# Row dot products for wq on VectorE, wq loaded in halves at its first use, and a kept group's slots spread, in a decode backward kernel

## The chip, the cores and the metric

The kernel runs on one core of one Trainium2 chip. The metric is device time in microseconds (us). A verdict of faster or slower needs 2%; intervals (95%) are given and used.

## The reference

Two layers of attention over a cached K and V and of an MLP, forward and backward, for one decoded token and a batch of 2. Cut to what matters:

```python
B, Sq, D = 2, 1, 1024
Hq, Hkv, Sk, Dh = 32, 4, 16384, 128          # 8 query heads share one KV head
q = (x @ wq)...                              # wq: 1024 x 4096
scores = einsum("bhqd,bhkd->bhqk", q, k) * Dh ** -0.5
o = einsum("bhqk,bhkd->bhqd", softmax(scores), v);   out = o.reshape(B, Sq, -1) @ wo
# x = x + A(layernorm(x)); x = x + B(layernorm(x)); both twice; then jax.vjp of all of it
```

The change lies in the attention backward of layer 1. For each of 8 groups g (batch row b, KV head kv; g = 4b + kv) it streams V (dP = dO V^T), makes dS, streams K (dq = dS K), and when both batch rows of a KV head have their dq, it adds that head's part of dn = dq wq^T.

## The kernel before

All weights, V and K pass through one pool of 1 MB tiles, `ld`, with NLD = 7 buffers. The last group (G - 1) keeps its K and V on chip, so its slots load nothing. A slot handles a quarter of a chunk: 8 transposes of 128x128 tiles of V, the 8 score matmuls of two slots earlier, and in every other slot 8 dq matmuls with K.

```python
slots = []
for i, g in enumerate(groups):                 # 0, 4, 3, 7, 1, 5, 2, 6
    for c in range(NCH):                       # 4 chunks of 1 MB
        for b in range(NB):                    # 4 slots to a chunk
            if g != G - 1:
                slots.append((g, c, b))
            if groups[(i + 1) % G] == G - 1:   # kept group beside the one before it
                slots.append((G - 1, c, b))
...
def finish(ps, g=g):                           # dq of group g is ready
    V.tensor_scalar(out=dqT[:, g, :], in0=ps, scalar1=QSCALE, scalar2=None, op0=ALU.mult)
    if groups.index(g) % 2 == 1:               # second batch row of a head
        wq_n[g % HKV][1]()                     # dq into dq_all
        if g != groups[-1]:
            wq_q.append(wq_n[g % HKV][3])      # the head's product, behind what is queued
        else:
            wq_n[g % HKV][3]()
...
if groups.index(g) % 2 == 1 and b == 1 and c == 1:
    n = wq_n[g % HKV] = wq_steps(...)
    for f in n[0]:                             # both halves of the head's wq: 2 x 1 MB, from ld
        f()
    wq_q.extend(n[2])                          # 8 row turns
...
if wq_q and s % 2 == 1:                        # one queued item in every other slot
    wq_q.popleft()()
```

A turn is 8 TensorE transposes of a 128x1024 row block and the copy back over it; the product then takes 8 row blocks x 8 matmuls of 32 columns. Copies out of PSUM (evacuations) go to ScalarE or VectorE, whichever has less booked in the balancer `load`; `charge` books time there:

```python
def pick():
    m = min(load.values())
    for k in load:
        load[k] -= m
    return "A" if load["A"] <= load["D"] else "D"
```

Of the kernel before, what the change touches and what calls it, by code (L numbers as in the profile page):

```python
# [9 lines left out]
BF16 = mybir.dt.bfloat16  # L10
F32 = mybir.dt.float32
I32 = mybir.dt.int32
ACT = mybir.ActivationFunctionType
ALU = mybir.AluOpType
# [9 lines left out]
def kernel(  # L24
# [25 lines left out]
    V = nc.vector  # L50
    S = nc.scalar
    PE = nc.tensor
# [39 lines left out]
    def pt(shape, dtype, name):  # L92
        return ps_tp.tile(shape, dtype, name=name, tag="tp")

    def px(shape, dtype, name):
        return ps_x.tile(shape, dtype, name=name, tag="x")
# [4 lines left out]
    def pm_(shape, dtype, name):  # L101
        return ps_sm.tile(shape, dtype, name=name, tag="sm")
# [34 lines left out]
    def charge(eng, us):  # L137
        load[eng] += us
# [7 lines left out]
    def evac_bf16(dst, src, n):  # L146
        if pick() == "A":
            S.copy(out=dst.bitcast(I32), in_=src.bitcast(I32))  # L148
            charge("A", 0.17 + n / 2 / 1200.0)
        else:  # L150
            V.tensor_copy(out=dst, in_=src)  # L151
            charge("D", 0.16 + n / 1920.0)
# [163 lines left out]
    class Ahead:  # L316
# [7 lines left out]
        def load(self, k):  # L324
            j0, rb = self.chunks[k]
            wv = w_load(self.W, j0, rb, D)
            for j in range(rb):
                self.rows[j0 + j] = wv[:, j, :]
# [9 lines left out]
        def products(self, j, out_ps, gT_bf):  # L338
            for o in range(8):
                PE.matmul(wide_out(out_ps, 2 * j), lhsT=self.rows[j][:, o * 128:(o + 1) * 128],  # L340
                          rhs=wide_in(gT_bf[:, o, :]), start=(o == 0), stop=(o == 7))
# [42 lines left out]
    class Acc:  # L384
# [3 lines left out]
        def __init__(self, g, src, coef, finish, half=0):  # L388
            self.g, self.src, self.coef, self.finish = g, src, coef, finish
            self.pre = {}  # L390
            self.cv = None
            self.acc = ACCT[:, half * 256:half * 256 + 256]
            self.half = half
            zero = lambda: V.memset(self.acc, 0.0)
            if half in Acc.in_use:
                Acc.then[half] = zero
            else:
                zero()
            Acc.in_use.add(half)
# [152 lines left out]
    def attn_bwd(l, do_bf, dqT, dn, groups, ahead):  # L552
        sch = Sched()
        wq_q, wq_n, w2_q = deque(), {}, deque()
        slots = []
        for i, g in enumerate(groups):
            for c in range(NCH):
                for b in range(NB):
                    if g != G - 1:
                        slots.append((g, c, b))  # L560
                    if groups[(i + 1) % G] == G - 1:
                        slots.append((G - 1, c, b))
        kTs, sc, accs = {}, {}, {}
        made = {"n": 0}

        def post(g, c):
            dp = sc.pop((g, c))
            PE.matmul(dp[:].rearrange("p h t -> p (h t)"), lhsT=hot3[:],
                      rhs=dlr[:, g, l, :].unsqueeze(2).to_broadcast([128, 8, TC]), start=False, stop=True)
            k = made["n"]  # L570
            made["n"] += 1
            ds = dXr[k // 2 % 3][:, :, k % 2]
            ev = e_all[:, g, c * CP:(c + 1) * CP, l, :, :].rearrange("p a h b -> p h a b")
            V.tensor_tensor(out=ds.rearrange("p a h b -> p h a b"),
                            in0=dp[:].rearrange("p h (a b) -> p h a b", b=2), in1=ev, op=ALU.mult)
            charge("D", 0.5)
            if c == 0:
                def finish(ps, g=g):
                    V.tensor_scalar(out=dqT[:, g, :], in0=ps, scalar1=QSCALE, scalar2=None, op0=ALU.mult)
                    if groups.index(g) % 2 == 1:  # L580
                        wq_n[g % HKV][1]()
                        if g != groups[-1]:
                            wq_q.append(wq_n[g % HKV][3])
                        else:
                            wq_n[g % HKV][3]()
                accs[g] = Acc(g, "K", None, finish, groups.index(g) % 2)
            acc = accs[g]
            if g == groups[-1]:
                accs[g].pre[c] = kv_load("K", g, c)
                if c == NCH - 1:  # L590
                    for k in range(NLD - 2):
                        ahead.load(k)
                        j0, rb = ahead.chunks[k]
                        w2_q.extend(lambda j=j: ahead.row(j) for j in range(j0, j0 + rb))
            coef = lambda u: ds[:, u - c * CP].rearrange("p h t -> p (h t)")
            sch.later(2, lambda: queue_acc(sch, acc, [c], c == NCH - 1, coef))

        def score(s):
            g, c, b = slots[s]
            if b == 0:  # L600
                sc[g, c] = px([128, 8, TC], F32, "dp")
            kT = kTs.pop(s)
            for j in range(8):
                PE.matmul(sc[g, c][:, :, b * 8 + j], lhsT=kT[:, j, :], rhs=do_bf[:, g, :], start=(b + j == 0),
                          stop=False)
            if b == NB - 1:
                post(g, c)

        cv = None
        s = 0  # L610
        v_turns = deque(lambda c=c, b=b: turn(held_tiles["V%d" % c][:, b * 1024:(b + 1) * 1024],
                                              lambda: pt([128, 8, 128], BF16, "turn"))
                        for c in range(NCH) for b in range(NB))
        while s < len(slots) + 2 or sch.busy():
            sch.s = s
            if s < len(slots):
                g, c, b = slots[s]
                if g == G - 1:
                    kTs[s] = kept_vT(c)[:, b * 8:(b + 1) * 8, :]
                else:  # L620
                    if b == 0:
                        cv = kv_load("V", g, c)
                    kTs[s] = emit_T(cv, b, True)
                    if s % 2 == 1 and v_turns:
                        v_turns.popleft()()
                if groups.index(g) % 2 == 1 and b == 1 and c == 1:
                    n = wq_n[g % HKV] = wq_steps(l, g % HKV, dqT, dn, lambda: pt([128, 8, 128], BF16, "wtq"),
                                                 lambda: px([128, 512], F32, "dn_ps"))
                    for f in n[0]:
                        f()  # L630
                    wq_q.extend(n[2])
            sch.run_slot(1 if s < len(slots) else 2)
            if 2 <= s < len(slots) + 2:
                score(s - 2)
            if wq_q and s % 2 == 1:
                wq_q.popleft()()
            s += 1
        return w2_q


# [148 lines left out]
    def wq_steps(l, kv, dqT, dn, new_tp, new_ps, get_=None, done_=lambda *job: None):  # L789

        hs = slice(kv * 8, kv * 8 + 8)
        box = {}

        def load(j):
            wt = ld.tile([128, LDW], BF16, name="wqt", tag="ld") if get_ is None else get_("wq", kv, j)
            box[j] = wt[:].rearrange("p (j n) -> p j n", j=4)
            if get_ is None:
                nc.sync.dma_start(box[j], wq_v[:, j:j + 4, kv * D:(kv + 1) * D])

        def turn_row(j):  # L800
            turn(box[j - j % 4][:, j % 4, :], new_tp)

        def products():
            ps = new_ps()
            for j in range(DJ):
                for o in range(8):
                    PE.matmul(wide_out(ps, 2 * j), lhsT=box[j - j % 4][:, j % 4, o * 128:(o + 1) * 128],  # L807
                              rhs=wide_in(dq_all[:, kv * 8 + o, 2 * l:2 * l + 2]), start=(o == 0), stop=(o == 7))
            V.tensor_tensor(out=dn[:], in0=dn[:], in1=ps[:, 0:2 * DJ].rearrange("p (j b) -> p j b", b=2), op=ALU.add)
            for j in (0, 4):  # L810
                done_("wq", kv, j)

        def dq_in():
            for b in range(2):
                V.tensor_copy(out=dq_all[:, hs, 2 * l + b], in_=dqT[:, b * HKV + kv, :])

        return [lambda j=j: load(j) for j in (0, 4)], dq_in, [lambda j=j: turn_row(j) for j in range(DJ)], products

    def attn_in_bwd(l, gT, dn, hook=lambda: None):
        sv = saved[f"a{l}"]  # L820
# [21 lines left out]
    fps = px([128, 512], F32, "w2b_f")  # L842
    V.memset(fps[:, 0:DJ * WIDE], 0.0)
    w2b = Ahead(B_w2, F, "w2b", h_all[:, :, lsl(1)], fps)
    rest = attn_bwd(1, do1, dq1, dn1, [b * HKV + kv for kv in (0, HKV - 1, *range(1, HKV - 1)) for b in range(2)], w2b)

    for k in range(NLD - 2, len(w2b.chunks)):
        w2b.load(k)
# [466 lines left out]
```

## Time and profile before

| | before |
|---|---|
| median (range) | 1181.85 us (1181.4 to 1183.74), 3 runs |
| layer-1 attention backward, by the trace | 512.8 us (dO in bf16) to 684.0 us (dn complete) |
| TensorE, VectorE, ScalarE, share of the span | 83%, 51%, 46% |
| mean HBM traffic | 379 GB/s; 413 to 423 in the best slices |

A row of the windows view lists busy us of PE (matmul), PEld (weight load), DVE (VectorE), ACT (ScalarE) and POOL, each with its number of instructions in brackets, then the granted TensorE clock, the DMA share, and GB/s. A row of the waits view reads "who and line <- what ended the wait: us in all, times, longest". The lines themselves are in the prediction.

### The profile page before, as it was taken

How to read it: one execution, taken by the hardware profiler on the slowest of the kernel's cores; microseconds unless marked ns; L12 is line 12 of the kernel's file. 1: busy time of each engine (PE TensorE's matmuls, PEld its weight loads, DVE VectorE, ACT ScalarE, POOL GpSimd, SP SyncE). 2: the span in 40 equal slices, each digit the busy share in tenths (PEclk: the TensorE clock that was granted, in tenths of full speed). 3: DMA queues.
4: the chain of work that ended last, by engine and by line, in shares of the span. 5: the costliest groups of instructions: out<-in, count | busy, mean ns of one | idle time of the engine just before them, and what ended most of it. 6: DMA issues, size and time to landing. Idle time of an engine off the chain costs nothing. (4 is left out here: it accounts for less than half of the span.)

```text
span 1179.9 us, 40673 instructions
## 1 busy us (share of the span) xinstructions
PE 975.0 (83%) x17981; PEld 750.0 (64%) x17981; DVE 606.4 (51%) x1262; ACT 539.1 (46%) x1368; POOL 63.9 (5%) x113
## 2 busy tenths in 40 slices
PE   4988894487879976899978689888898889999786
PEld 3866673487767755888767588755555554555452
DVE  1544351233545423454323235557777878786774
ACT  0544341022535420344323234357767767786673
POOL 0000000000000000000000000001111111111111
PEclk9988795597989875899989899978767877786785
DMA  9999999989999989989899999767999999999996
GB/s 370 415 417 417 417 417 395 395 337 364 418 417 416 414 311 416 371 322 380 316 396 398 365 335 368 287 236 279 394 407 413 418 417 421 419 420 420 423 423 269
DMA packets 89133, 449.35 MB, mean 381 GB/s; under 512 B 7026, under 2 KB 7026, under 8 KB 49788
## 3 DMA queue, kind: packets, MB, share of 16 engines
q1 hardware_dynamic: 72204, 348.17, 74.5%
q0 software_dynamic: 16752, 98.59, 20.3%
q8 instruction: 140, 2.29, 0.8%
q14 instruction: 37, 0.30, 0.1%
HBM read 348.14 MB, written 98.58 MB: 379 GB/s over the span
## 5 line engine op out<-in xcount | busy, mean ns | idle before, releaser
L148 ACT COPY kT<-tp 128x512 int32<-128x512 int32 x176 | 103.4, 588 | 272.3 <-PE tp L379 263.0
L151 DVE COPY kT<-tp 128x1024 bf16<-128x1024 bf16 x192 | 131.3, 691 | 153.7 <-PE tp L379 143.1
L379 PE MATMUL tp<-ident,kv_K 128*128 128x128 bf16 x1728 | 145.8, 234 | 3.6 <-DMA kv_K<-in_A_k_cache_dram 3.6
L379 PEld LDWEIGHTS <-kv_K 128*128 128x128 bf16 x1728 | 110.6, 104 | 4.4 <-DMA kv_K<-in_A_k_cache_dram 4.1
L156 ACT CAST big<-xm 128x512 bf16<-128x512 f32 (+1 forms) x163 | 88.9, 593 | 26.5 <-PE xm L976 14.4
L159 DVE CAST big<-xm 128x512 bf16<-128x512 f32 (+1 forms) x134 | 87.2, 685 | 23.7 <-PE xm L1117 10.9
L532 PEld LDWEIGHTS <-kT 128*128 128x128 bf16 x2048 | 76.4, 98 | 28.1 <-issue 22.0
L532 PE MATMUL sc<-qT_bf,kT 128*128 128x8 bf16 x2048 | 92.0, 171 | 0.5 <-issue 0.4
L263 PE MATMUL wtp<-ident,wt 128*128 128x128 bf16 x928 | 77.4, 232 | 5.3 <-issue 4.0
L297 PEld LDWEIGHTS <-wt 128*128 128x128 bf16 x1696 | 49.0, 104 | 46.7 <-issue 14.9
L496 ACT ACTIVATE e_all<-sc,negm 128x64 bf16<-128x64 f32 x256 | 77.2, 345 | 1.1 <-DVE negm L491 1.1
L379 PE MATMUL tp<-ident,kv_V 128*128 128x128 bf16 x864 | 68.2, 223 | 6.2 <-DMA kv_V<-in_A_v_cache_dram 4.0
L411 PE MATMUL acc_all<-kv_V,e_all 128*16 128x256 bf16 x864 | 46.3, 294 | 29.4 <-DMA kv_V<-in_A_v_cache_dram 16.1
L159 DVE CAST keepK<-xm 128x512 bf16<-128x512 f32 x93 | 60.4, 685 | 18.2 <-PE xm L1117 14.0
L148 ACT COPY wT<-wtp 128x512 int32<-128x512 int32 (+1 forms) x60 | 34.3, 572 | 71.8 <-PE wtp L263 62.2
L151 DVE COPY wT<-wtp 128x1024 bf16<-128x1024 bf16 (+1 forms) x64 | 40.7, 640 | 51.1 <-PE wtp L263 47.5
L156 ACT CAST keepK<-xm 128x512 bf16<-128x512 f32 x104 | 56.2, 592 | 21.7 <-PE xm L1117 20.6
L263 PEld LDWEIGHTS <-wt 128*128 128x128 bf16 x928 | 59.4, 104 | 5.9 <-issue 4.5
L156 ACT CAST keepV<-xm 128x512 bf16<-128x512 f32 (+1 forms) x93 | 50.4, 594 | 24.7 <-PE xm L1117 22.6
L159 DVE CAST keepV<-xm 128x512 bf16<-128x512 f32 (+1 forms) x79 | 51.8, 685 | 16.2 <-PE xm L1117 12.4
L496 ACT ACTIVATION_READ_ACCUMULATOR e_all<-sc,negm 128x1 f32 x256 | 60.1, 235 | 0.0
L379 PEld LDWEIGHTS <-kv_V 128*128 128x128 bf16 x864 | 53.4, 100 | 7.7 <-DMA kv_V<-in_A_v_cache_dram 4.4
(325 smaller groups left out, 1758.0 us busy)
## 6 DMA issues: line engine op xcount, KB each, us to landing
kv_K<-in_A_k_cache_dram SPq DMA_DIRECT2D x81, 1024.0 KB, 13.1
kv_V<-in_A_v_cache_dram SPq DMA_DIRECT2D x81, 1024.0 KB, 12.2
out_dram<-big POOLq DMA_DIRECT2D x36, 1024.0 KB, 15.8
wt<-in_A_wo_dram SPq DMA_DIRECT2D x32, 1024.0 KB, 10.3
wt<-in_B_w_dram SPq DMA_DIRECT2D x32, 896.0 KB, 14.3
out_dram<-keepK POOLq DMA_DIRECT2D x22, 1024.0 KB, 15.8
out_dram<-keepV POOLq DMA_DIRECT2D x18, 1024.0 KB, 16.2
wt<-in_A_wq_dram SPq DMA_DIRECT2D x16, 1024.0 KB, 9.2
```

The lines of the kernel that those rows point to most:

```text
L148: S.copy(out=dst.bitcast(I32), in_=src.bitcast(I32))
L151: V.tensor_copy(out=dst, in_=src)
L156: S.copy(out=dst, in_=src)
L159: V.tensor_copy(out=dst, in_=src)
L263: PE.transpose(tp[:, o, :], wv[:, j, (o0 + o) * 128:(o0 + o + 1) * 128], ident[:])
L297: PE.matmul(fps[:, jo, :].rearrange("p (a b) -> p a b", b=2), lhsT=wv[:, j, jo * 128:(jo + 1) * 128], rhs=xT_bf[:, j0 + j, :].unsqueeze(1) ...
L379: PE.transpose(tp[:, j, :], cv[:, b * 8 + j, :], ident[:])
L411: PE.matmul(self.acc[cg:cg + 16, :], lhsT=coef(u), rhs=self.cv[:, t:t + 2, :].rearrange("p t d -> p (t d)"), start=False, stop=True, tile_ ...
L496: S.activation(out=e_all[:, g, f * half:(f + 1) * half, l, h, :], in_=sc[g][f][:, h, :].rearrange("p (a b) -> p a b", b=2), func=ACT.Exp, ...
L532: PE.matmul(sc[g][f][:, :, t % TH], lhsT=kT[:, j, :], rhs=q_bf[:, g, :], start=True, stop=True)
```

## The change

The intent: take wq work off TensorE, which looks full, and give it to VectorE, which is half idle; and hold load buffers for wq for less time. Five of the eight half-heads (20 of 32 row blocks) become dot products on VectorE. Each half is loaded when its first dot or turn is emitted. The kept group's slots are spread over two groups and it gets an accumulator of its own. With more than six wq items queued, one is taken in every slot instead of in every other one.

```diff
-                    if g != G - 1:
-                        slots.append((g, c, b))
-                    if groups[(i + 1) % G] == G - 1:
-                        slots.append((G - 1, c, b))
+                    slots.append((g, c, b))
+                    if 2 <= i < 2 + NCH // 2 and c % 2 == 0:
+                        slots.append((G - 1, (i - 2) * 2 + c // 2, b))
...
+        def dot(kv, n, j, b):
+            V.scalar_tensor_tensor(out=junk[:], in0=n[4][j - j % 4][:, j % 4, :], scalar=1.0,
+                                   in1=dqb[b][:].rearrange("p o d -> p (o d)"), op0=ALU.mult, op1=ALU.mult,
+                                   accum_out=dnp[:, kv, j, b:b + 1])
+            charge("D", 1.15)
+            if b == 1:
+                V.tensor_tensor(out=dn[:, j], in0=dn[:, j], in1=dnp[:, kv, j], op=ALU.add)
+        def spread(kv, b):          # dq of one batch row to all partitions: 8 transposes, 1 copy
...
+        def by_dots(kv):            # called when both batch rows of a head have their dq
+            nj = DJ // 2 if kv == groups[-3] % HKV else DJ      # head 1: half on TensorE
...
+            def item(j, b):
+                if j % 4 == 0 and b == 0:
+                    n[0][j // 4]()  # load this half now
+                dot(kv, n, j, b)
...
-                    if groups.index(g) % 2 == 1:
+                    done_g.append(g % HKV)
+                    if g == groups[-1]:
                         wq_n[g % HKV][1]()
-                        if g != groups[-1]:
-                            wq_q.append(wq_n[g % HKV][3])
-                        else:
-                            wq_n[g % HKV][3]()
-                accs[g] = Acc(g, "K", None, finish, groups.index(g) % 2)
+                        wq_n[g % HKV][3]()
+                    elif done_g.count(g % HKV) == 2:
+                        by_dots(g % HKV)
+                accs[g] = Acc(g, "K", None, finish, 2 if g == G - 1 else groups.index(g) % 2)
...
-            if wq_q and s % 2 == 1:
+            if wq_q and (s % 2 == 1 or len(wq_q) > 6):
                 wq_q.popleft()()
+            if dots and s % 3 < 2:
+                dots.popleft()()
```

More of the change, by code (lines that the diff above doesn't have):

```diff
@@ L391, in __init__ @@
             self.cv = None
-            self.acc = ACCT[:, half * 256:half * 256 + 256]
+            self.acc = ACCT[:, half * 256:half * 256 + 256] if half < 2 else pm_([128, 256], F32, "acc2")[:]
             self.half = half
@@ L558, in attn_bwd @@
                 for b in range(NB):
-                    if g != G - 1:
-                        slots.append((g, c, b))
-                    if groups[(i + 1) % G] == G - 1:
-                        slots.append((G - 1, c, b))
+                    slots.append((g, c, b))
+                    if 2 <= i < 2 + NCH // 2 and c % 2 == 0:
+                        slots.append((G - 1, (i - 2) * 2 + c // 2, b))
         kTs, sc, accs = {}, {}, {}
         made = {"n": 0}
+        done_g = []
+        dots = deque()
+        dqb = [ktp.tile([128, 2 * NB, 128], BF16, name="dqb", tag="blk", bufs=2) for _ in range(2)]
+        junk = wrk.tile([128, D], BF16, name="junk", tag="rowout")
+        dnp = vec.tile([128, HKV, DJ, 2], F32, name="dnp")
+        def dot(kv, n, j, b):
[6 more added lines that the diff above has]
+        def spread(kv, b):
+            tp = pt([128, 8, 128], BF16, "dqr")
+            for o in range(8):
+                PE.transpose(tp[:, o, :], dq_all[:, kv * 8 + o, 2 * l + b:2 * l + b + 1].to_broadcast([128, 128]), ident[:])
+            evac_bf16(dqb[b][:].rearrange("p a b -> p (a b)"), tp[:].rearrange("p a b -> p (a b)"), 1024)
+        def by_dots(kv):
+            n = wq_n[kv] = wq_steps(l, kv, dqT, dn, lambda: pt([128, 8, 128], BF16, "wtq"),
+                                    lambda: px([128, 512], F32, "dn_ps"))
+            nj = DJ // 2 if kv == groups[-3] % HKV else DJ
+            n[1]()
+            for b in range(2):
+                wq_q.append(lambda b=b: spread(kv, b))
+            def item(j, b):
+                if j % 4 == 0 and b == 0:
+                    n[0][j // 4]()
+                dot(kv, n, j, b)
+            wq_q.append(lambda: dots.extend(lambda j=j, b=b: item(j, b) for j in range(nj) for b in range(2)))
+            if nj < DJ:
+                wq_q.append(lambda: (n[0][1](), n[2][nj]()))
+                wq_q.extend(n[2][nj + 1:])
+                wq_q.append(lambda: n[3](nj))
         def post(g, c):
@@ L625, in attn_bwd @@
                         v_turns.popleft()()
-                if groups.index(g) % 2 == 1 and b == 1 and c == 1:
+                if g == groups[-1] and b == 1 and c == 0:
                     n = wq_n[g % HKV] = wq_steps(l, g % HKV, dqT, dn, lambda: pt([128, 8, 128], BF16, "wtq"),
                                                  lambda: px([128, 512], F32, "dn_ps"))
-                    for f in n[0]:
-                        f()
-                    wq_q.extend(n[2])
+                    for k, f in enumerate(n[0]):
+                        wq_q.append(lambda f=f, k=k, n=n: (f(), n[2][4 * k]()))
+                        wq_q.extend(n[2][4 * k + 1:4 * k + 4])
             sch.run_slot(1 if s < len(slots) else 2)
@@ L634, in attn_bwd @@
                 score(s - 2)
-            if wq_q and s % 2 == 1:
+            if wq_q and (s % 2 == 1 or len(wq_q) > 6):
                 wq_q.popleft()()
+            if dots and s % 3 < 2:
+                dots.popleft()()
             s += 1
+        assert not dots and not wq_q
         return w2_q
@@ L801, in turn_row, with products @@
             turn(box[j - j % 4][:, j % 4, :], new_tp)
-        def products():
+        def products(j0=0):
             ps = new_ps()
-            for j in range(DJ):
+            for j in range(j0, DJ):
                 for o in range(8):
@@ L808, in products @@
                               rhs=wide_in(dq_all[:, kv * 8 + o, 2 * l:2 * l + 2]), start=(o == 0), stop=(o == 7))
-            V.tensor_tensor(out=dn[:], in0=dn[:], in1=ps[:, 0:2 * DJ].rearrange("p (j b) -> p j b", b=2), op=ALU.add)
+            V.tensor_tensor(out=dn[:, j0:DJ], in0=dn[:, j0:DJ],
+                            in1=ps[:, 2 * j0:2 * DJ].rearrange("p (j b) -> p j b", b=2), op=ALU.add)
             for j in (0, 4):
@@ L815, in dq_in @@
                 V.tensor_copy(out=dq_all[:, hs, 2 * l + b], in_=dqT[:, b * HKV + kv, :])
-        return [lambda j=j: load(j) for j in (0, 4)], dq_in, [lambda j=j: turn_row(j) for j in range(DJ)], products
+        return [lambda j=j: load(j) for j in (0, 4)], dq_in, [lambda j=j: turn_row(j) for j in range(DJ)], products, box
     def attn_in_bwd(l, gT, dn, hook=lambda: None):
@@ L844 @@
     w2b = Ahead(B_w2, F, "w2b", h_all[:, :, lsl(1)], fps)
-    rest = attn_bwd(1, do1, dq1, dn1, [b * HKV + kv for kv in (0, HKV - 1, *range(1, HKV - 1)) for b in range(2)], w2b)
+    rest = attn_bwd(1, do1, dq1, dn1, [b * HKV + kv for kv in (0, HKV - 1, *range(1, HKV - 1)) for b in range(2)
+                                     if b * HKV + kv != G - 1], w2b)
     for k in range(NLD - 2, len(w2b.chunks)):
```

## The prediction

> **What bounds the kernel now.** I started from the page's picture of 40 slices (29.5 us each), to see which stages have the DMA at its ceiling.
>
> ```profile
> PE   4988894487879976899978689888898889999786
> DVE  1544351233545423454323235557777878786774
> DMA  9999999989999989989899999767999999999996
> GB/s 370 415 417 417 417 417 395 395 337 364 418 417 416 414 311 416 371 322 380 316 396 398 365 335 368 287 236 279 394 407 413 418 417 421 419 420 420 423 423 269
> ```
>
> In most slices 413 to 423 GB/s flow: that is the ceiling that this kernel reaches. The attention backward of layer 1, the only place the diff touches, lies at about 513 to 684 us (slices 17 to 23): 316 to 398 GB/s with TensorE at 7 to 9 tenths. So there is something to win here, but only the gap between these rates and the ceiling. Next I cut that stretch into parts, and into pieces of 3 us where the rate was lowest. The columns are the busy us of PE, PEld, DVE, ACT, POOL, the granted clock, the DMA share, and GB/s.
>
> ```profile
> 523.00:580.00 57.00, 54.40 (x1195) 45.78 (x1192) 24.28 (x47) 23.04 (x41) 0.00 (x0) 1.00 0.91 336
> 580.00:664.00 84.00, 65.45 (x1391) 54.14 (x1390) 25.89 (x56) 24.39 (x43) 0.00 (x0) 0.92 1.00 398
> 664.00:679.00 15.00, 14.18 (x287) 11.97 (x287) 5.50 (x10) 5.23 (x10) 0.00 (x0) 0.88 0.89 323
> ```
> ```profile
> 568.00:571.00 3.00, 3.00 (x72) 2.36 (x70) 0.76 (x3) 1.67 (x3) 0.00 (x0) 1.00 0.47 183
> 571.00:574.00 3.00, 3.00 (x77) 2.55 (x73) 1.00 (x3) 1.06 (x2) 0.00 (x0) 1.00 0.33 68
> ```
>
> So the stage has two limits. From 523 to 580 TensorE is busy 54.4 of 57 us and the DMA gets 336 GB/s. From 580 to 664 the DMA is never idle (share 1.00, 398 GB/s), and TensorE waits. VectorE is busy about 43% or less throughout. The DMA's worst hole is 565 to 574 us. The waits of the DMA-issuing queue (490 to 690 us) say what refused it a buffer:
>
> ```profile
> SPq L368 <- PE tp L379: 60.9, 21, 10.8
> SPq L368 <- PE acc_all L411: 49.7, 19, 7.1
> SPq L368 <- PE dn_ps L807: 12.4, 4, 4.6
> ```
>
> L807 is the wq product: four times a K or V load waited for it, since wq shares the seven 1 MB load buffers with K and V. The issue times of wq and the TensorE timeline show how long it keeps them:
>
> ```profile
> 525.59 4.46 SPq L798 DMA_DIRECT2D wqt<-in_A_wq_dram  x2
> 551.67 2.55 SPq L798 DMA_DIRECT2D wqt<-in_A_wq_dram  x2
> ```
> ```profile
> 572.89 0.61 PE L313 MATMUL wtq<-ident,wqt 128*128 128x128 bf16 x8
> 573.33 0.61 PE L379 MATMUL tp<-ident,kv_V 128*128 128x128 bf16 x8
> ...
> 576.56 1.76 PE L807 MATMUL dn_ps<-dq_all,wqt 128*128 128x32 bf16 x64
> 580.04 0.61 PE L379 MATMUL tp<-ident,kv_V 128*128 128x128 bf16 x8 [1.72 <-issue]
> ```
>
> Head 0's two wq buffers are taken at 525.6 and given back after the product at 576.6; head 3's two are taken at 551.7. Between 552 and 577 wq therefore holds four of seven buffers. The code says why: the product is appended to the same queue as the next head's eight turns, and waits behind them (walking the loop by hand: turns in slots 21 to 35, product in slot 59 of 128). The V load behind the pause at 578.3 to 580.0 was issued only at 572.7; at the 7.8 us median that V loads take to land here, it fits. The profile calls this pause "issue", so that reading is mine.
>
> **What the Trainium skill says.** "VectorE: DVE Perf Modes", section "The perf-mode tier table": a bf16 tensor_tensor from SBUF can run at 2x, tensor_reduce at 1x only; it has no row for a scalar_tensor_tensor with an accumulator. I assume 1x. The trace agrees with a 1x slope where it has one: 128x64 f32 tensor_tensor takes 218 ns and 128x256 takes 421 ns, 1.06 ns an element. "TensorE: Matmul & The Clock Gate", section "Back-to-back issue gap", gives about 81 ns per matmul at N=128 in a stream of weight loads and matmuls; this trace is faster (8 transposes start 0.44 us before the next group, 55 ns each), so I use the trace. "Perfetto Trace Analysis", section "Optimization Strategy": consistent bubbles on the engine that should be saturated can mean too few buffers for the next tile. The hole at 565 to 574 us agrees.
>
> **The change part by part.**
> *TensorE, removed.* 20 of 32 wq row blocks lose their turn (8 transposes, 0.44 us) and their product (8 matmuls; a head's 64 take 1.74 us, so 0.22 us): 20 x 0.66 = 13.2 us. *Added:* for three heads and two batch rows, 8 transposes that spread dq over all partitions: 6 x 0.44 = 2.6 us. Net 10.6 us less.
> *Evacuations.* 20 go and 6 come, about 0.6 to 0.7 us each: some 9 us less on ScalarE and VectorE together.
> *VectorE, added.* 20 row blocks x 2 batch rows = 40 dots of 1024 elements. From the 256-element tensor_tensor: 421 + 768 x 1.06 = 1.23 us; the diff itself books 1.15. So 46 to 49 us. VectorE was busy 62.6 of the 170 us from 513 to 683, so it comes to about 110, or 65%. Locally, at most two dots fall in three slots: 2.5 us against three slots of 1.29 us (165 us over 128 slots). With the 0.42 us dS product of every fourth slot that nearly fills it, and the balancer, which is charged for the dots, sends the evacuations to ScalarE (three of 0.59 us in 3.9 us fit).
> *Buffers.* A half is loaded when its first dot or turn is emitted and freed after its last, some 12 slots later. In my walk through the loop, head 0 now holds one buffer in slots 49 to 61 and one in 61 to 72, where heads 0 and 3 had held two to four from slot 21 to 77.
> *Moved.* The 16 slots of the kept group, which load no V or K, were all interleaved with one group (32 slots with little DMA work). They are now spread over two groups (24 slots each), which evens TensorE work per byte. They need a third accumulator; it gets its own PSUM bank, and nothing else here uses that bank.
>
> *On the path.* From 523 to 580 the before moved 336 x 57 = 19.2 MB. At 398 GB/s, the rate of the DMA-bound part next to it, that takes 48.1 us. TensorE must fit under it: 54.4 us, less 16 turns (7.0), less the product and pause (3.4), less some eight kept slots moved to the next group (8 x 0.37 = 3.0), plus two spreads (0.9) gives 42. It fits, so the DMA becomes the bound: 57 - 48.1 = **8.9 us** won. From 580 to 664 nothing is won: same bytes, same rate. The tail (664 to 684) keeps its last loads, eight turns and 64 products of the last head. In my walk the last dot falls in slot 126 of 128, so the dots do not lengthen it. I take off 1 us for dots that hold up an evacuation. Everything later shifts as a block: after 685 us the diff touches nothing. Sum: 1181.85 - 8 = **about 1174 us**.
>
> **The rivals.**
> (1) *VectorE becomes the bound.* A dot waiting for its wq half blocks every evacuation behind it, and TensorE with it. For it: VectorE runs in order, and loads here take 8 to 13 us to land. Against it: V and K too are loaded where they are first used, in the same queue order, so a wq half lands one load (2.6 us) after its neighbour, and there are four transposed-tile buffers. If it held, the gain would shrink to 0 to 4 us: 1178 to 1182, or 1185 at worst.
> (2) *The transfer was the limit anyway.* wq is still 8 MB; if the rate does not rise above 336 GB/s for another reason, little is won: 1179 to 1182. Against it: 398 GB/s right afterwards with the same kind of loads.
> (3) *More than expected.* If the whole stage rose to about 413 GB/s, 523 to 679 (57.5 MB by the 3 us windows) would take 139 instead of 156 us: 17 us, 1165 us. The later part is against it: it stays at 398 with the DMA never idle.
> (4) *The last group gets crowded.* Head 1's wq now falls there too, so it loads 15 MB instead of 13. That is the same total later in the stage; but if the last loads arrive late, 2 to 5 us come back.
>
> **Range and chances.** Even the largest gain, 17 us, is 1.4%, short of 2% (23.6 us). A loss over 2% would need VectorE to hold up nearly every slot. So within 2%: 0.96; faster 0.02; slower 0.02. The range runs from 1167 (most of rival 3) to 1181 (rivals 1 or 4 taking nearly everything).
>
> **What would show it.** (a) The dots take 1.15 to 1.3 us each, 46 to 52 us in all. (b) No wait of a load on the wq product in mid-stage; the hole at 565 to 574 us is gone, and no 3 us window before the tail falls under 250 GB/s. (c) The windows from about 525 us to the tail all show a DMA share near 1.0 and some 400 GB/s. (d) The last wq product, at 682.0 us before, comes at about 674; from there every event is the same 8 us early. The prediction is wrong if the dots wait long for wq with TensorE waiting on VectorE, if the DMA share stays under 0.95 with TensorE busy, or if the gain at the last wq product is lost again after 685 us.

## The result

In the first comparison the changed kernel took 1173.44 us (median of 4 runs, 1170.99 to 1173.91) against 1181.62 us before (4 runs): ratio 0.9929, interval 0.9902 to 0.9955. Two later comparisons gave less: 1176.74 against 1180.31 us (0.9963, 0.9947 to 0.998) and 1179.78 against 1181.35 us (0.997, 0.9941 to 0.9999). So the gain is real but small, 0.3 to 0.7%.

The 40 slices of the changed kernel, for the lines shown of before:

```profile
PE   4988885497879876899987889888898999898886
DVE  1544451133545433454845434567777877886774
DMA  9999999998999989989999989677999999999996
GB/s 370 415 417 416 418 417 396 395 356 351 416 417 413 416 329 416 390 320 398 387 410 411 352 320 338 254 271 322 361 403 419 414 417 421 418 421 418 422 423 263
```

Slices 18 to 21 (counted from 0) carry 387 to 411 GB/s where before had 316 to 398, and VectorE is at 8 tenths in slice 19. The same three windows as in the prediction, and the weakest stretch in mid-stage:

```profile
523.00:580.00 57.00, 54.21 (x1190) 44.80 (x1188) 35.07 (x71) 24.71 (x44) 0.00 (x0) 0.99 0.98 385
580.00:664.00 84.00, 67.10 (x1276) 54.64 (x1274) 42.53 (x98) 38.96 (x71) 0.00 (x0) 0.86 0.99 397
664.00:679.00 15.00, 14.06 (x326) 12.05 (x319) 2.57 (x15) 7.33 (x14) 0.00 (x0) 0.89 0.98 369
```
```profile
565.00:568.00 3.00, 2.70 (x63) 2.19 (x62) 2.96 (x7) 1.48 (x4) 0.00 (x0) 1.00 0.74 243
568.00:571.00 3.00, 3.00 (x77) 2.18 (x73) 2.75 (x7) 1.15 (x2) 0.00 (x0) 1.00 0.90 363
```

The first window rose from 336 to 385 GB/s, with TensorE as busy as before: 54.21 us against 54.40. So TensorE did not get free; it did other work. The same window with only TensorE's instructions on wq (turns and products), before and after, and then with only those that read the loaded V (its transposes), before and after. These rows have one busy column, TensorE's:

```profile
523.00:580.00 57.00, 11.47 (x192) 1.00 0.91 336
523.00:580.00 57.00, 0.00 (x0) 0.99 0.98 385
```
```profile
523.00:580.00 57.00, 19.90 (x262) 1.00 0.91 336
523.00:580.00 57.00, 25.64 (x339) 0.99 0.98 385
```

The 11.5 us of wq work left this window and K and V work took its place. In the trace of before, TensorE waits in these 57 us for only 0.4 us for anything that the profile names. The waits of the DMA-issuing queue (490 to 690 us) show another surprise:

```profile
SPq L368 <- PE acc_all L411: 48.4, 19, 6.8
SPq L368 <- PE tp L379: 47.0, 21, 5.9
...
SPq L368 <- DVE dn L576: 12.7, 5, 4.6
```

K and V loads used to wait 12.4 us for the wq product; they now wait 12.7 us for the last dot of a half (L576 is the sum behind it). The wait changed its owner, not its size (`dn` is the gradient that the dots add into). The dots themselves, from the groups of VectorE instructions from 513 to 690 us:

```profile
L571 DVE SCALAR_TENSOR_TENSOR junk<-wqt,dqb 128x1024 bf16<-128x1024 bf16 x40 | 48.7, 1218 | 5.6 <-DMA wqt<-in_A_wq_dram 5.3
...
L571 DVE DVE_READ_ACCUMULATOR junk<-wqt,dqb 128x1 f32 x40 | 3.3, 82 | 0.0
```

To see where time goes, I cut every trace at the same events: the stage runs from the bf16 copy of dO to the first use of the finished dn; then everything to the end of the span. "DMA idle" sums (1 - share) over the 3 us windows below 1, for 523 to 649 us and for 649 to 682 us.

| trace | stage, us | from there to the end, us | DMA idle mid, us | DMA idle late, us |
|---|---|---|---|---|
| before | 171.2 | 495.9 | 6.8 | 1.9 |
| after (three traces) | 163.9, 166.2, 167.7 | 498.2, 503.1, 501.6 | 2.1, 2.0, 2.8 | 2.3, 5.2, 4.5 |

So the stage is 3.5 to 7.3 us shorter, and part of that is lost again after it, in code that the diff does not touch. In the first pair of traces, whose spans differ by 7.8 us, chance helped: the changed kernel entered the stage 2.8 us earlier (510.0 against 512.8 us), through code that is the same in both.

### The profile page after: what moved, and what is told of

Its sections match the earlier page's. It is cut to its first block, busy times and chain, and to the rows that moved or that the text cites. A ratio compares the mean times of both kernels' runs of the same rounds, so it can differ in the third digit from the quotient of the medians. Undisturbed runs are those within 1.5% of the kernel's fastest.

```text
span 1172.1 us, 40218 instructions
## 1 busy us (share of the span) xinstructions
PE 968.7 (83%) x17709; PEld 743.1 (63%) x17709; DVE 627.2 (54%) x1319; ACT 555.1 (47%) x1395; POOL 63.9 (5%) x113
## 5 line engine op out<-in xcount | busy, mean ns | idle before, releaser
L148 ACT COPY kT<-tp 128x512 int32<-128x512 int32 x204 | 120.0, 588 | 254.5 <-PE tp L379 246.6
L151 DVE COPY kT<-tp 128x1024 bf16<-128x1024 bf16 x164 | 112.1, 690 | 117.1 <-PE tp L379 106.9
L159 DVE CAST big<-xm 128x512 bf16<-128x512 f32 x141 | 91.9, 686 | 33.6 <-PE xm L1018 15.9
L156 ACT CAST big<-xm 128x512 bf16<-128x512 f32 x156 | 84.8, 595 | 24.2 <-PE xm L1018 14.7
L379 PE MATMUL tp<-ident,kv_V 128*128 128x128 bf16 x864 | 72.9, 233 | 9.9 <-DMA kv_V<-in_A_v_cache_dram 8.3
L297 PEld LDWEIGHTS <-wt 128*128 128x128 bf16 x1696 | 48.9, 103 | 45.8 <-issue 14.7
L379 PEld LDWEIGHTS <-kv_V 128*128 128x128 bf16 x864 | 57.5, 104 | 11.8 <-DMA kv_V<-in_A_v_cache_dram 9.2
L156 ACT CAST keepV<-xm 128x512 bf16<-128x512 f32 (+1 forms) x98 | 53.3, 595 | 20.3 <-PE xm L1159 17.0
L159 DVE CAST keepV<-xm 128x512 bf16<-128x512 f32 (+1 forms) x74 | 48.5, 686 | 20.3 <-PE xm L1159 16.1
```

Of the source, the lines that this page charges most:

```text
L148: S.copy(out=dst.bitcast(I32), in_=src.bitcast(I32))
L151: V.tensor_copy(out=dst, in_=src)
L156: S.copy(out=dst, in_=src)
L159: V.tensor_copy(out=dst, in_=src)
L297: PE.matmul(fps[:, jo, :].rearrange("p (a b) -> p a b", b=2), lhsT=wv[:, j, jo * 128:(jo + 1) * 128], rhs=xT_bf[:, j0 + j, :].unsqueeze(1) ...
L379: PE.transpose(tp[:, j, :], cv[:, b * 8 + j, :], ident[:])
```

## The experiments

The change has three parts: **slots** (the kept group spread over two groups), **late halves** (wq loaded in halves where it is first used), and **dots** (VectorE instead of TensorE). My theory by now was that buffers make the gain; the rival, that the relief of TensorE makes it. A third possibility was not given a run of its own: late halves also do the wq work on TensorE later, in a stretch where TensorE has room. The twelve runs went in three calls of four, each run with 5 timed rounds and a profile. All passed the comparison with the reference.

**The changed kernel again.** No edit.

> The changed kernel again, unedited, as the yardstick for the other runs and to see what differs between two traces of one kernel. All theories: 0.5 to 0.9% faster than before (1171 to 1176 us). If the 3 us between 701 and 752 us that the first trace gave back come back here too, they belong to the change; if that stretch takes about 48 us as in the kernel before, they are scatter of one execution.

Measured: 1176.74 us against 1180.31, 0.9963 (0.9947 to 0.998). The first comparison was on the lucky side. After the stage, the stretch from the hidden gradient of layer 0's MLP to the bf16 copy of layer 0's dO (the w1 and wo passes) took 50.9 us in this trace, 51.4 in the first, and 48.3 before. So the 3 us that the first trace lost there were lost again.

**Product first.** The kernel before; a finished head's product goes ahead of the next head's turns.

```diff
-                            wq_q.append(wq_n[g % HKV][3])
+                            wq_q.appendleft(wq_n[g % HKV][3])
```

> The kernel before, with one word changed: a finished head's wq product goes to the front of the queue and not behind the next head's turns, so head 0 gives its two load buffers back some 14 slots (about 14 us) earlier; all work stays on TensorE. Theory buffers (the gain comes from wq no longer holding load buffers): the DMA hole at 565 to 574 us goes and 3 to 5 us of the 8 are won, 1177 to 1179. Rival TensorE work (the gain comes from the 10.6 us of TensorE work taken away): 0 to 1 us won, 1181 to 1182.

Measured: 1178.74 against 1180.31, 0.9985 (0.9967 to 1.0002), not clear of zero. Head 0's product did move, from 576.6 to 561.7 us. The hole of 565 to 574 us did not go; it shrank and spread:

```profile
568.00:571.00 3.00, 3.00 (x73) 2.36 (x71) 0.99 (x2) 1.56 (x3) 0.00 (x0) 1.00 1.03 426
571.00:574.00 3.00, 2.56 (x62) 2.11 (x59) 0.69 (x1) 0.70 (x2) 0.00 (x0) 1.00 0.61 183
574.00:577.00 3.00, 3.00 (x71) 2.34 (x69) 1.45 (x3) 1.56 (x3) 0.00 (x0) 1.00 0.84 322
577.00:580.00 3.00, 3.00 (x79) 2.36 (x76) 1.15 (x2) 0.69 (x2) 0.00 (x0) 1.00 0.82 317
```

Neither theory does well here. Freeing two buffers earlier won little. Two reasons fit, and no run parts them: the buffers were held beside the kept group's slots, which need no loads; and TensorE was full in that stretch (54.7 of 57 us from 523 to 580 us, with the same 128 turn transposes as before), so loads that come sooner find it no freer.

**Slots alone.** The kernel before with the new order of slots and the third accumulator; wq still in early pairs, all on TensorE.

```diff
+                    slots.append((g, c, b))
+                    if 2 <= i < 2 + NCH // 2 and c % 2 == 0:
+                        slots.append((G - 1, (i - 2) * 2 + c // 2, b))
...
+        wq_at = {4: 0, 1: 3, 5: 1, 6: 2}      # group that triggers a head's loads
-                if groups.index(g) % 2 == 1 and b == 1 and c == 1:
+                if g in wq_at and b == 1 and c == 1:
```

> Of the change only the order of slots: the kept group spread over two groups, with its own accumulator; wq as before, loaded early as pairs, turned and multiplied on TensorE. Theory buffers: the spread also takes away the clash of head 0's product with head 3's turns, so 2 to 5 us won, 1177 to 1180. Rival TensorE work: only the evening out helps, 0 to 2 us, 1180 to 1182. If the order of slots is nearly all of the gain: 7 to 8 us, 1174.

Measured: 1188.59 against 1180.31, 1.0067 (1.0042 to 1.0093): 8 us slower, which no theory had expected. The stage took 175.1 us. Its windows (580 to 650 us, and two of 3 us), and what TensorE waited for from 595 to 632 us:

```profile
580.00:650.00 70.00, 56.12 (x1155) 47.17 (x1153) 22.79 (x50) 21.35 (x37) 0.00 (x0) 0.89 0.88 342
606.00:609.00 3.00, 2.21 (x40) 1.73 (x40) 0.00 (x0) 0.59 (x1) 0.00 (x0) 0.81 0.45 156
618.00:621.00 3.00, 2.75 (x56) 2.34 (x56) 1.08 (x3) 1.74 (x3) 0.00 (x0) 1.00 0.39 85
```
```profile
PE acc_all L411 <- DMA kv_K<-in_A_k_cache_dram: 7.4, 3, 3.9
```

The DMA engines stood idle and then TensorE waited for K loads that had been issued late. With the kept group's slots gone from beside them, the early pairs of heads 3 and 1 (issued at 568.8 and 594.8 us) sit in slots that nearly all need K and V (by a walk through the loop, all but four kept slots beside head 3's). That is consistent with the buffers: the place of the holding would matter, not only its length. No run moves the place alone, so this much is argued.

**Slots and late halves, all on TensorE.** The changed kernel without dots: in each half, load, four turns, and the product of those four rows.

```diff
-            for b in range(2):
-                wq_q.append(lambda b=b: spread(kv, b))
-            ... dots.extend(...)
+            for k in range(2):
+                wq_q.append(lambda k=k: (n[0][k](), n[2][4 * k]()))
+                wq_q.extend(n[2][4 * k + 1:4 * k + 4])
+                wq_q.append(lambda k=k: n[3](4 * k, 4 * k + 4))
```

> The changed kernel with all wq work back on TensorE: same slots, same late loads in halves, each half turned and multiplied at once and then given back; no dots on VectorE. Theory buffers: as fast as the change, 1172 to 1175, since the DMA is the bound there. Rival TensorE work: 13 us of TensorE work come back, 4 to 8 us slower than the change, 1178 to 1182.

Measured: 1171.65 against 1180.31, 0.9929 (0.9912 to 0.9946). It is faster than the changed kernel (1176.74). The stage took 165.9 us, as in the changed kernel. All wq work is on TensorE, and the gain is there in full. Against slots alone, only the way that wq is loaded, queued and given back differs, and the two do about the same wq work on TensorE from 523 to 580 us (128 instructions each) at about the same rate (374 and 378 GB/s). The late halves are 17 us faster (1171.65 against 1188.59), and the difference opens from 580 to 650 us: 405 GB/s against 342. So with the new slots the reading that fits is the buffers: loads wait for one while TensorE waits for loads. The parts of late halves (the later load, the return in halves, the faster queue) were not tried one by one.

**Early loads.** The changed kernel with dots and new slots, but both halves of heads 0, 3 and 1 loaded early as before and held.

```diff
-                if j % 4 == 0 and b == 0:
-                    n[0][j // 4]()
...
+                if g in (4, 1, 5) and b == 1 and c == 1:
+                    kv = {4: 0, 1: 3, 5: 1}[g]
+                    n = wq_n[kv] = wq_steps(...)
+                    for f in n[0]:
+                        f()
```

> The changed kernel with one part undone: both halves of a head's wq are loaded together at the points where the kernel before loaded them, and held until the dots are done; the dots stay on VectorE. Theory buffers: two to four of seven buffers are held for long again, so most of the gain goes, or more: 1179 to 1188. Rival TensorE work: the gain stays, 1172 to 1175.

Measured: 1193.93 against 1180.08, 1.0129 (1.0099 to 1.0159), 14 us slower than before although TensorE has its relief. The stage took 181.8 us and 580 to 650 us carries:

```profile
580.00:650.00 70.00, 49.94 (x871) 40.10 (x872) 26.89 (x65) 24.62 (x45) 0.00 (x0) 0.77 0.86 330
```

TensorE is at 71% and the DMA at 0.86; TensorE waits 21.8 us of these 70 for K and V loads. The changed kernel differs only in the late loads. So with the new slots the relief does not carry the gain: without the late loads there is a loss. The relief with the old slots and early loads was not run.

**Old slots.** The changed kernel with the old order of slots (the slot loop, two accumulators and the list of groups as before).

> The changed kernel with the old order of slots (the kept group all beside one group, two accumulators); dots and late halves stay. If the spread of the slots matters for itself: 2 to 4 us slower than the change, 1175 to 1178. If the buffers or the TensorE work alone make the gain: 1172 to 1175.

Measured: 1177.74 against 1180.08, 0.998 (0.9959 to 1.0). The changed kernel, on the same chip, had 0.9963. It was run at another time. By the timed runs that difference is not clear; the stage in the trace is 168.5 us.

**Short dots.** Every dot reads 16 of 1024 elements. The result is wrong (it passed the comparison all the same); loads, waits and bookings stay.

```diff
-            V.scalar_tensor_tensor(out=junk[:], in0=n[4][j - j % 4][:, j % 4, :], scalar=1.0,
-                                   in1=dqb[b][:].rearrange("p o d -> p (o d)"), ...
+            V.scalar_tensor_tensor(out=junk[:, 0:16], in0=n[4][j - j % 4][:, j % 4, 0:16], scalar=1.0,
+                                   in1=dqb[b][:, 0, 0:16], ...
```

> The changed kernel with every dot cut to 16 of 1024 elements (wrong result on purpose, out_1 only or little more), so VectorE loses some 45 us of work; loads and waits for them stay. If the dots hold nothing up (my sum took off 1 us for them): 1172 to 1174. If VectorE has become a bound: 3 to 5 us faster than the change, 1168 to 1170.

Measured: 1176.93 against 1180.08, 0.9962 (0.994 to 0.9984), the same ratio as the changed kernel's. A dot took 166 ns (median), so 42 us of VectorE work were gone, and in 580 to 650 us VectorE fell from 35.15 to 11.25 us at an unchanged DMA rate:

```profile
580.00:650.00 70.00, 56.34 (x1092) 45.67 (x1092) 11.25 (x74) 31.44 (x57) 0.00 (x0) 0.85 1.02 411
```

So the dots' own time holds nothing up that these runs can resolve.

**Dots twice.** The same kernel with every dot done twice.

```diff
+            for _ in range(2):
                 V.scalar_tensor_tensor(out=junk[:], ...)
                 charge("D", 1.15)
```

> The changed kernel with every dot done twice (same result): 49 us more of VectorE work, which is then more than full while dots run. If VectorE has room to spare: at most 2 us slower, up to 1176. If it is close to its limit there: 5 to 20 us slower, 1178 to 1193.

Measured: 1190.38 against 1180.08, 1.0088 (1.0069 to 1.0107). VectorE is busy 83% of the stretch and TensorE now waits for it (waits of 550 to 670 us; `dX` is dS):

```profile
580.00:650.00 70.00, 46.85 (x895) 38.13 (x893) 58.36 (x119) 25.94 (x47) 0.00 (x0) 0.82 0.83 322
```
```profile
PE tp L379 <- DVE dX L612: 8.4, 1, 8.4
...
PE acc_all L411 <- DVE dX L612: 3.0, 2, 2.3
```

There is room for 49 us of dots, not for 98.

**The changed kernel, third time.**

> The changed kernel unedited, a third time, since its gain was 0.7% in the first comparison and 0.4% in the second. If 0.4% is its true size against the kernel before: 0.995 to 0.998 again. If the first was right: 0.991 to 0.995.

Measured: 1179.78 against 1181.35, 0.997 (0.9941 to 0.9999); its six runs spread over 10 us.

**Slots and late halves on TensorE, again.**

> Changed slots and late halves, all wq work on TensorE, again, next to the changed kernel. If the dots cost more than they bring: 3 to 6 us faster than the changed kernel of this call once more. If the difference was scatter: within 2 us of it.

Measured: 1172.4 against 1181.35, 0.9929 (0.9902 to 0.9956), the same as the first time, and again faster than the changed kernel beside it (by the means of 6 runs, 1172.56 against 1178.25 us). The stage took 164.3 us. This is the fastest version. Its stretch of 580 to 650 us has all the wq work on TensorE and the DMA full:

```profile
580.00:650.00 70.00, 61.83 (x1312) 51.48 (x1311) 26.05 (x56) 24.94 (x45) 0.00 (x0) 0.98 1.02 409
```

**Late halves alone.** The kernel of the last run with the old order of slots.

> The late halves alone: the old order of slots, all wq work on TensorE. If the late halves make the gain and the order of slots only adds to it: 2 to 6 us faster than before, 0.995 to 0.998. If late halves bring nothing without the spread of slots: 0.999 to 1.004. If they do all of it: as fast as the run with spread slots.

Measured: 1175.88 against 1181.35, 0.9957 (0.9927 to 0.9988). Late halves alone are faster than before; the stage took 168.3 us. With the spread of slots it was 165.9 and 164.3.

**Balance reset.** The changed kernel; the balancer's sums, which stand at 0.38 (ScalarE) and 3.59 us (VectorE) after the dots when the program emits the kernel, are set to zero after the stage.

```diff
+    load["A"] = load["D"] = 0.0
     charge("D", 2.0)
     g2 = attn_in_bwd(1, g3, dn1, lambda: some(rest, 2))
```

> The changed kernel with one line: the balancer's two sums are set to zero after the attention backward, where the dots leave VectorE booked 3.2 us ahead and the next evacuations therefore go to ScalarE. If this leftover is what the dots cost downstream (the w1 and wo stretch took 50 to 51 us in both traces of the changed kernel and 47 to 48 in those with all wq on TensorE): 2 to 3 us faster than the changed kernel of this call, and that stretch back to 47 to 48. If not: within 1 us of it.

Measured: 1174.85 against 1181.35, 0.9945 (0.9917 to 0.9973). That is 3 us faster by the means than the changed kernel beside it (1175.30 against 1178.25), but the intervals overlap: inconclusive by the timed runs. In the trace the w1 and wo stretch took 48.6 us (50.1 in the changed kernel).

The same cuts for these runs:

| trace | slots | late | dots | stage, us | from there to the end, us |
|---|---|---|---|---|---|
| before | | | | 171.2 | 495.9 |
| product first | | | | 170.6 | 498.3 |
| slots alone | x | | | 175.1 | 494.8 |
| late halves alone | | x | | 168.3 | 492.1 |
| slots + late (two traces) | x | x | | 165.9, 164.3 | 492.8, 491.6 |
| late + dots (old slots) | | x | x | 168.5 | 499.0 |
| slots + dots (early loads) | x | | x | 181.8 | 497.2 |
| after (three traces) | x | x | x | 163.9, 166.2, 167.7 | 498.2, 503.1, 501.6 |
| after, dots short | x | x | x | 165.4 | 497.7 |
| after, dots twice | x | x | x | 182.7 | 493.0 |
| after, balance reset | x | x | x | 165.9 | 493.8 |

## Why the prediction was right or wrong

The time was right: about 1174 us, and 1173.44, 1176.74 and 1179.78 us came out, all inside 1167 to 1181, all within 2%. That the first came so close is partly luck: by the three ratios the gain is 0.71, 0.37 and 0.30%, or 8.4, 4.4 and 3.5 us, against 8 forecast. Of the reasons, the two limits held, the offload proved unnecessary, and several terms were off.

*The ceiling held.* The stage is bound by loads over most of its length once they are issued in time. The window of 523 to 580 us rose to 385 GB/s, near the 398 assumed, and 580 to 650 us carries 410. The stage won 7.3 us in the first trace, 5.0 and 3.5 in the others, against 7.9 expected.

*"TensorE must fit under it": right as a limit, but VectorE was not needed for it.* From 523 to 580 us TensorE was full in all fourteen traces, 53.0 to 55.2 us of 57, and the rate is higher where less wq work lies in the window:

| trace | TensorE on wq, 523 to 580 us | TensorE transposing V, us | GB/s |
|---|---|---|---|
| before; product first | 11.5; 11.6 | 19.9; 19.9 | 336; 352 |
| late halves alone | 6.9 | 22.4 | 372 |
| slots + late (two traces) | 6.8, 6.8 | 22.7, 23.2 | 374, 373 |
| slots alone | 6.6 | 23.5 | 378 |
| after (first trace) | 0 | 25.6 | 385 |

The prediction saw one way to get it out, onto VectorE. Late halves with all wq work on TensorE get nearly as far by doing part of it later, after 580 us, where TensorE had 10 of 70 us free before. The 10.6 us net that the dots took off TensorE then won no more: the stage took 165.9 and 164.3 us without the dots, and TensorE was busy for about 149 us of it; with them it took 163.9 to 167.7 us, TensorE was busy for 140 to 143, and the rest became idle time. With the relief kept and the late halves undone the stage takes 181.8 us. So the late halves make the gain, in the company of the new slots.

The 42 us was also summed wrongly: the pause of 1.7 us is idle time and not in the 54.4 busy us, and of the eight kept slots that were to leave, one left this window (104 score matmuls with the kept V before, 96 after, 8 to a slot). With both put right it is about 46 us, which still fits under 48.1.

*The queue was not the cause of the hole.* The four buffers held from 552 to 577 us were read rightly, but giving two of them back 15 us earlier won 0.15%, not clear of zero. In the two windows of the hole that the prediction shows, TensorE was busy for 3.00 of 3.00 us. The prediction booked the spread of the slots as an even gain for TensorE; in truth it is a loss with early pairs (0.67%) and of use only with late halves (stage 168.3 to about 165). What late halves win with the old slots (0.43%) can be buffers or the later TensorE work: from 580 to 650 us the rate hardly moved (396 to 401 GB/s), and no run parts the two. With the new slots the buffers fit: in the runs "slots alone" and "early loads", TensorE and the DMA engines both stand idle for part of 580 to 650 us (DMA share 0.88 and 0.86).

*"At 664 to 684 the tail keeps its shape" was too kind.* Rival 4 came in part: head 1's wq now falls into the last group, and in the second trace the DMA engines stand idle before the stage's end, 5.2 us after 649 us where before had 1.9:

```profile
661.00:664.00 3.00, 0.00 (x0) 0.00 (x0) 1.15 (x3) 0.00 (x0) 0.00 (x0) 0.60 0.64 187
664.00:667.00 3.00, 1.77 (x16) 1.62 (x16) 0.00 (x0) 0.59 (x1) 0.00 (x0) 0.50 0.68 283
667.00:670.00 3.00, 3.00 (x62) 2.19 (x64) 0.00 (x0) 1.76 (x3) 0.00 (x0) 0.76 0.31 62
```

*"Everything later shifts as a block" was wrong.* From the finished dn to the end the three traces of the changed kernel took 498.2 to 503.1 us, those of late halves on TensorE (old or new slots) 491.6 to 492.8, and before 495.9. The diff changes no line there, but the balancer enters that code with other sums and so can deal the evacuations differently. Setting the sums to zero gave 493.8 us in one trace. That points to the balancer, but the times do not settle it. Before, "product first" and late halves alone enter that code with the same sums (0.15 us for ScalarE and 0.42 for VectorE when the program is emitted) and took 495.9, 498.3 and 492.1 us, so 6 us lie between traces that the sums do not tell apart. The run with dots twice speaks against a simple rule: it leaves 49.6 us booked to VectorE and took 493.0. What the dots cost after the stage stays open in its mechanism; that the version without dots is faster has been measured.

*Of the checks:* (a) hit: 1218 ns a dot, 48.7 us in all. (b) half hit: the hole went, one window stood at 243 GB/s against my 250, and the loads' wait for wq did not vanish but moved to the dots, 12.7 us. (c) hit until about 650 us. (d) half hit: the last wq product, at 682.0 us before, started at 671.8, 674.4 and 676.4 us in the three traces against about 674, helped by an earlier entry into the stage (2.8, 2.6 and 2.1 us); the "same 8 us from there on" failed. Rival 1 (VectorE in the way) is refuted at this size by the short dots and came true at double. Rival 2 is refuted by the 385 GB/s of the first window.

## What to carry to other kernels

When loads share a small ring of buffers, ask for each tile from which slot to which slot it is held, and whether those slots need loads themselves: with the new slots, loading wq late instead of early was worth 17 us, and moving 10 us of work to another engine nothing on top. Where an engine is full in one stretch and has room in the next, doing its work later can free it as well as another engine can: before you move work off it, try the version that leaves it there and changes only when it is loaded and done. When a busy share does not move, look at what the engine is busy with. And look past the end of the stage you changed: a balancer with a memory carries the change into code that the diff leaves alone, whether or not its cost can be measured.

## What the Trainium skill lacked or had wrong

- "VectorE: DVE Perf Modes", "The perf-mode tier table", has no row for scalar_tensor_tensor with an accumulator. From SBUF in bf16 it took 1217 ns for 1024 elements and 166 ns for 16, so (1217 - 166) / 1008 = 1.04 ns an element: no faster than the 1.06 ns that the prediction took from the f32 tensor_tensor. The accumulator read is a second instruction of 82 ns, as the page's section "Two Vector instructions with no wait between them" says.
- "TensorE: Matmul & The Clock Gate", "Back-to-back issue gap", gives about 81 ns per matmul at N=128 in a stream with weight loads. Here transposes of 128 columns came every 55 ns (8 in 0.44 us), also with a weight load each. That is close to what the section gives for an isolated matmul (128 / 2.4 + 2.5, about 56 ns) and says under-counts such a stream. The wq product's pairs at N=32 came every 27 ns (64 in 1.74 us).
- "Perfetto Trace Analysis", "Identifying the Most-Contended Engine", warns that matmul busy time does not tell how near TensorE is to its roofline, and recommends the weight loads' busy share. No run here shows the one measure to be better than the other: from 523 to 580 us matmul busy time was 54.4 and 54.2 of 57 us, the weight loads 45.8 and 44.8, at 336 and at 385 GB/s. What the section lacks for such a case is to split the busy time by what it is spent on: 11.5 us of it on wq before, none after.
